# mLSTM cell and exact-GELU feed-forward on one core: y of two batches in chunks three to six turned by VectorE and a way through DRAM, and the down stage's steps in a new order

## The chip, the cores and the metric

The kernel runs on one core of a Trainium2 chip. The core has TensorE (matrix products, PE in the profile), VectorE (DVE), ScalarE (ACT), GpSimd (POOL) and SyncE (SP), whose queue issues nearly all DMAs of this kernel. Each engine works through its own instructions in program order; they wait for one another by semaphores. The metric is the device time of one execution in microseconds, as the median of several runs. A share of the executions is recorded by the hardware profiler, and times of single instructions come from one such execution.

## The reference

An mLSTM cell runs over 768 steps for 4 batches of 8 heads of 40, and its output, 3072 rows of 320, goes through a feed-forward block with an exact GELU.

```python
for t in range(S):
    m_new = np.maximum(f_gate[:, :, t] + m, i_gate[:, :, t])
    f_stab = np.exp(f_gate[:, :, t] + m - m_new)
    i_stab = np.exp(i_gate[:, :, t] - m_new)
    C = f_stab * C + i_stab * einsum(v_t, k_t)
    n = f_stab * n + i_stab * k_t
    denom = np.maximum(np.abs(n . q_t), 1.0)
    y[:, :, t] = sigmoid(o_gate[:, :, t]) * (C q_t) / denom
...
h = x @ w_in                                   # x: (3072, 320), w_in: (320, 2048)
g = 0.5 * h * (1.0 + erf(h * inv_sqrt2))
return g @ w_out                               # w_out: (2048, 320)
```

All data are float32.

## The kernel before

The 768 steps are cut into six chunks of 128, and in each chunk the recurrence is computed in parallel form: scores of queries and keys, weighted by exponentials of the gates, times the values, plus what the state of the chunk before contributes. A chunk of all four batches is 512 tokens, which then go through the feed-forward block together. The product with `w_in` (the *up* stage) takes each float32 operand in parts: `x_hi`, `x_lo` and `x_all` (L499 to L516 make them) against `w_in_hi`, `w_in_lo` and their sum `w_mid`. The product with `w_out` (the *down* stage) is done with seven half-size products instead of eight, each for two tiles of tokens: 14 steps F of eight matrix products (L877).

The program is played from lists of words. After each up stage of chunk c, `DOWN` is played: the 14 steps F of chunk c, with all steps of the cell of chunk c + 1 spread between them. This happens four times, for the cells of chunks three to six (c = 2 to 5 in the code). The cell of chunk two is played within `FRONT`, and after the last up stage there are 14 F alone. The word order is the order of the instructions on every engine's queue. The letters, with the two pairs of batches u = 0, 1 and the two halves j = 0, 1 of a chunk:

- M u: GpSimd masks the loaded gate rows (L530). W b: ScalarE takes their exponentials (L540).
- K b, Q b: VectorE turns keys and queries of batch b by 32x32 blocks (L552); Q also has GpSimd weigh the values (L434). K and Q of batches 0 and 1 are played inside the up stage.
- L 3: GpSimd clears two regions of the old `g` (L149) and SP loads keys and queries of batch 3 there (L159, eight DMAs). j: eight such loads for the next chunk.
- S u: TensorE makes the scores (L588), VectorE multiplies them by the weights (L591).
- r u,j: TensorE reads the state (L602), VectorE multiplies by the decay (L615).
- C u: TensorE makes the state's update (L637). a u,j: GpSimd decays the state (L623). b u,j: VectorE adds the update (L645).
- V u: TensorE multiplies weights and values (L655), into the PSUM banks that C used (tag "a"); VectorE adds the state's part (L666); SP loads the next gate rows (L175), keys and values (L133).
- G b: ScalarE makes the output gate (L417, L419). Y b (`finish`): GpSimd and VectorE gate and normalise y (L475 to L482). For one batch at a time, VectorE then copies the last 64 columns twice into `y_rest` (L488).
- X b (`turn_y`): TensorE turns y in three transposes into the PSUM tile `px` (L499), ScalarE writes `x_hi` (L509), SP loads the next output gates (L138, two DMAs).
- R b (`split_x`): VectorE makes `x_lo` and `x_all` from `px` and `x_hi` (L515, L516).
- N: VectorE's late sums for the down products (L907); F11 to F14 need them. After F's, ScalarE copies (L894, L900) or VectorE adds (L890) the results, and SP sends them out (L862).

The up stage that follows needs `x_hi` of all four batches at once, then `x_lo`, then `x_all`.

Of the kernel before, what the change touches and what calls it, by code (L numbers as in the profile page):

```python
# [9 lines left out]
F32 = mybir.dt.float32  # L10
F32R = mybir.dt.float32r
BF16 = mybir.dt.bfloat16
U32 = mybir.dt.uint32
AF = mybir.ActivationFunctionType
OP = mybir.AluOpType

P = 128

I23 = 2.0 ** 23
PART = 1.0 - 2.0 ** -13  # L20
# [5 lines left out]


FRONT = """w0 L0 t0 w1 L1 O0 O1 P0 k2 E s0 w3 I4 t2 P1 g1 v0 L3 e2 t1 O3 g0 K N D O2 s1 w2 t3 y0 s2 c1 L5 M0 g3 K g2 v1 y1 P2 J Q s3 c0 L4 W0 v2 c3 x0 y2 j1,0 j1,1 x1 P3 O4 J c2 v3 K y3 O5 x2 W1 J A P7 q d P8 P9 x3 a0,0 K J K j0,1 K u0 J G0 j0,0 U J u1 C0 b0,0 O7 r0,0 a0,1 b0,1 H K S0 r0,1 K J K u3 J K L6 J A A J K K J e3 K J K J J K K J K J L7 z J a1,0 A U K J K J K J K j2,0 z K j2,1 O6 J U U h J h p K j3,1 J K J K j3,0 J F F M1 V0 u2 K J W3 h z z h Y0 W2 z z S1 r1,0 C1 z F z F Z G1 b1,0 F F F X0 a1,1 b1,1 G2 Y1 F r1,1 n z V1 F F X1 G3 Y2 R0 R1 Y3 F F X2 R2 F X3 e4 e5 e6 Z F R3"""
DOWN = """F M0 W0 W1 F G2 S0 G1 L3 r0,0 a0,0 C0 K2 M1 b0,0 F W2 F F a0,1 b0,1 K3 r0,1 G0 V0 W3 F Q2 F a1,0 Y0 Y1 Q3 F S1 r1,0 C1 b1,0 X0 F X1 a1,1 R0 b1,1 N j F r1,1 V1 G3 Y2 Y3 R1 F F X2 F X3 R2 F R3"""


@with_exitstack
def kernel(
# [16 lines left out]
    nc = tc.nc  # L50

    B, H, S, D = q.shape
    L = P
# [5 lines left out]
    DM = H * D  # L59
    DFF = moe_w_in.shape[1]  # L60
    NF = DFF // P
    TG = B * L
    R = P // 2
    NX = 2
    NLD = 4
# [10 lines left out]
    raw = ctx.enter_context(tc.tile_pool(name="raw", bufs=2))  # L76
    two = ctx.enter_context(tc.tile_pool(name="two", bufs=2))
    dram = ctx.enter_context(tc.tile_pool(name="dram", bufs=1, space=bass.MemoryType.DRAM))
# [23 lines left out]
    odd_far = blocks[:, H * XB:]  # L102
# [9 lines left out]
    ob = [const.tile([P, DM], F32, name=f"ob{n}") for n in range(NLD)]  # L112
# [3 lines left out]
    f_sb = gates.tile([BH, NCH, L], F32, name="f_sb")  # L116
    i_sb = gates.tile([BH, NCH, L], F32, name="i_sb")
    M_d = dram.tile([NCH - 1, 2, BH, R], F32, name="M_d")

    def out_of(n):  # L120
        return ob[n % NLD].rearrange("p (h d) -> p h d", d=D)

    halves = (slice(0, R), slice(R, P))
    quarters = tuple(slice(R // 2 * n, R // 2 * (n + 1)) for n in range(4))

    def load(n, first=0, end=4):

        if n >= NCH * B:
            return
        c, b = divmod(n, B)  # L130
        for src, dst in ((q, qb), (k, kb), (v, vb), (o_gate, None))[first:end]:
            if dst or c < 1:
                nc.sync.dma_start(out=dst[turn_of(n)][:, :, 0:D] if dst else out_of(n), in_=src[b, :, c * L:(c + 1) * L, :].rearrange("h p d -> p h d"))  # L133
                continue
            u, j = divmod(b, 2)
            t = c * L + R * j
            for i in range(2):
                nc.sync.dma_start(out=out_of(n)[halves[i]], in_=src[2 * u + i, :, t:t + R, :].rearrange("h p d -> p h d"))  # L138
# [24 lines left out]
    def turn_of(n):  # L163

        return n % NLD if n < 2 * B else (n - 2 * B) % NQ
# [214 lines left out]
    def unread(bank):  # L380
        for _ in range(idle[0]):
            nc.tensor.matmul(bank, ident, ident, start=True, stop=True, skip_group_check=True)
        idle[0] = 0
# [4 lines left out]
    class FirstCell:  # L388


        def __init__(self, c):
            self.c = c

            self.engine = nc.gpsimd
            self.finished, self.turned = [], []
            self.qT, self.kT, self.vw, self.far, self.hs, self.px = {}, {}, {}, {}, {}, {}
# [74 lines left out]
        def finish(self, b):  # L471
            n, hs = self.c * B + b, self.hs.pop(b)
            y = out_of(n)
            if self.c > 0:
                nc.gpsimd.tensor_tensor(out=y, in0=hs[:, :, 0:D], in1=y, op=OP.mult)  # L475
            else:
                nc.vector.scalar_tensor_tensor(out=y, in0=y, scalar=1.0, in1=hs[:, :, 0:D], op0=OP.add, op1=OP.mult)
            den = two.tile([P, H], F32, name="den", tag="den", bufs=1)
            nc.vector.tensor_scalar(out=den, in0=hs[:, :, D], scalar1=-1.0, scalar2=None, op0=OP.mult)
            nc.vector.scalar_tensor_tensor(out=den, in0=hs[:, :, D], scalar=1.0, in1=den, op0=OP.max, op1=OP.max)  # L480
            nc.vector.reciprocal(out=den, in_=den)
            nc.vector.scalar_tensor_tensor(out=y, in0=y, scalar=0.5 if self.c < 1 else 1.0, in1=den.unsqueeze(2).to_broadcast([P, H, D]), op0=OP.mult, op1=OP.mult)  # L482
            self.finished.append(b)
            if len(self.finished) == len(self.turned) + 1:
                self.twice(b)
# [3 lines left out]

        def turn_y(self, b):  # L490
            n, t = self.c * B + b, slice(b * L, (b + 1) * L)
            if self.c > 0:
                px = ps_tr.tile([P, NX + 1, L], F32, name="px", tag="tr")
            else:
                px = ps_mm.tile([P, NX + 1, L], F32, name="px", tag="b")
            unread(px[:, 0, :])
            for k in range(NX + 1):
                y = ob[n % NLD][:, k * P:(k + 1) * P] if k < NX else y_rest.rearrange("p two r -> p (two r)")
                nc.tensor.transpose(px[:, k, :], y, ident)  # L499
            self.turned.append(b)  # L500
            if len(self.finished) > len(self.turned):
                self.twice(b + 1)
            if self.c == 0:
                nc.scalar.copy(out=first_x[:, :, t], in_=px)
                return
            self.px[b] = px
            if "x" not in parts:
                parts["x"] = raw.tile([P, NX + 1, TG], F32R, name="x_hi", tag="x", bufs=1)
            nc.scalar.activation(out=parts["x"][:, :, t], in_=px, func=AF.Copy, scale=PART)  # L509
            load(n + NLD, 3, 4)  # L510

        def split_x(self, b):
            px, t = self.px.pop(b), slice(b * L, (b + 1) * L)
            hi = parts["x"][:, :, t]
            nc.vector.scalar_tensor_tensor(out=parts["x_lo"][:, :, t], in0=px, scalar=-1.0 / BASE, in1=hi, op0=OP.mult, op1=OP.add)  # L515
            nc.vector.tensor_tensor(out=parts["x_all"][:, :, t], in0=px, in1=hi, op=OP.subtract)  # L516

# [160 lines left out]
    w_sums, parts, fars, w_hi, w_lo, w_mid = [], {}, [], [], [], {}  # L678
# [261 lines left out]
    def in_turn(steps):  # L940
        todo = list(steps)
        return lambda: todo.pop(0)() if todo else None

    def first_steps(letters):
        cell = FirstCell(0)
        return dict(zip(letters, (cell.weights, cell.gate, cell.turn, cell.scores, cell.carry, cell.values, cell.finish, cell.turn_y)))

    def cell_steps(c, letters, before):
        cell = Cell(c)
        cell.before = before  # L950
        return dict(zip(letters, (cell.mask, cell.weights, cell.gate, cell.scores, cell.update, cell.values,
                                  cell.finish, cell.turn_y, cell.split_x, cell.read, cell.decayed, cell.grown, cell.load_last,
                                  cell.turn_k, cell.turn_q, cell.load_next, cell.first_turn, cell.weigh_values)))

    first_g = Hidden()
    first_products, first_late = down_steps(0, first_g)
    n_pieces = range(len(pieces))
    last_of = lambda c0, c1: by_sub(gg)[:, c0:c1, :, R - 1:R].rearrange("p c j l -> p (c j) l")
    dec_of = lambda c0, c1: dec[:, 2 * (c0 - 1):min(2 * (c1 - 1), 2 * (NCH - 1) - 1)]
    steps = first_steps("wgtscvyx") | cell_steps(1, "MWGSCVYXRrab---pju", first_g)  # L960
    steps |= dict(P=fetch, L=lambda n: load(n, 0, 2), O=lambda n: load(n, 2, 4), e=load_M, E=second_gates,
                  N=later_gates, I=keep_clock, k=warm, D=lambda: gates_turned((ew[:, 0:2], ewT[:, 0:2])),
                  Q=lambda: (gates_turned((ew[:, 2:], ewT[:, 2:])), decays_turned(2, NCH)),
                  d=lambda: (decays_turned(1, 2), decays_last(last_of(1, 2), dec_of(1, 2))),
                  q=lambda: decays_last(last_of(2, NCH)[:, 0:-1], dec_of(2, NCH)),
                  A=in_turn(first_up_steps(0)), U=in_turn(first_up_steps(1)), F=in_turn(first_products), n=first_late,
                  h=in_turn(lambda k=k: hidden_sums(first_g, 2 * k, 2 * k + 2) for k in range(HF // 2)),
                  z=in_turn(lambda w=w: weight_sum(*w) for w in sums),
# [3 lines left out]
    for c in range(1, NCH):  # L972
        g, steps = Hidden(), {}
        if c + 1 < NCH:
            steps = cell_steps(c + 1, "MWGSCVYXRrabLKQj", g)
        up(g, [lambda b=b: (steps["K"](b), steps["Q"](b)) for b in range(2)] if steps else [])
        products, late = down_steps(c, g)
        steps |= dict(F=in_turn(products), N=late)
        play("F " * 14 if c + 1 == NCH else DOWN, steps)

# [29 lines left out]
```

## Time and profile before

| | us |
|---|---|
| runs | 454.77, 455.12, 455.23: median 455.12 |
| the profiled execution, its own time | 453.08 |
| its span, first to last instruction | 451.1 |
| TensorE busy in the span | 444.3 |
| VectorE busy | 301.8 |
| ScalarE busy | 188.7 |
| GpSimd busy | 76.7 |
| all transposes of y by TensorE (72, L499) | 9.6 + 6.6 |
| a down stage, start of its first F to start of the next up stage | 40.0 |

The span is what the profiler records between the first and the last instruction; the execution's time has about 2 us around it. A row of a timeline gives start, duration, engine, line, operation, the tile written and the tiles read, and how many instructions were merged into it. In a row of windows, each engine's busy time is followed by its number of instructions, then come TensorE's granted clock (1.00 is full), the share of the DMA engines that was busy and GB/s. A row of DMA issues gives the number of DMAs, the size of each and the median time in us from issue to landing. TensorE's matrix products overlap and their ends are modelled, so its work is best measured from start to start.

### The profile page before, as it was taken

How to read it: one execution, taken by the hardware profiler on the slowest of the kernel's cores; microseconds unless marked ns; L12 is line 12 of the kernel's file. 1: busy time of each engine (PE TensorE's matmuls, PEld its weight loads, DVE VectorE, ACT ScalarE, POOL GpSimd, SP SyncE). 2: the span in 40 equal slices, each digit the busy share in tenths (PEclk: the TensorE clock that was granted, in tenths of full speed). 3: DMA queues.
4: the chain of work that ended last, by engine and by line, in shares of the span. 5: the costliest groups of instructions: out<-in, count | busy, mean ns of one | idle time of the engine just before them, and what ended most of it. 6: DMA issues, size and time to landing. Idle time of an engine off the chain costs nothing.

```text
span 451.1 us, 12699 instructions
## 1 busy us (share of the span) xinstructions
PE 444.3 (98%) x5256; PEld 394.8 (88%) x5256; DVE 301.8 (67%) x596; ACT 188.7 (42%) x476; POOL 76.7 (17%) x118
## 2 busy tenths in 40 slices
PE   8999999999999999999999999999999999999996
PEld 4897888999878999878999878999877999877996
DVE  4995779897967789645779635779544779532331
ACT  5989597813246811135901134901133911232100
POOL 2222120012200522200522300522200421000000
PEclk9999999999999999999999999999999999999999
DMA  9999999422822257512256522256522300200002
GB/s 157 211 199 229 275 265 227 75 45 57 192 47 55 52 120 150 122 42 51 55 113 148 122 53 51 55 108 118 111 52 51 69 16 3 60 0 1 0 1 58
DMA packets 112808, 43.04 MB, mean 95 GB/s; under 512 B 87600, under 2 KB 107056, under 8 KB 112752
## 3 DMA queue, kind: packets, MB, share of 16 engines
q1 hardware_dynamic: 112432, 41.92, 41.7%
q8 instruction: 41, 0.67, 0.6%
q10 hardware_dynamic: 320, 0.33, 0.2%
q14 instruction: 15, 0.12, 0.1%
HBM read 38.21 MB, written 4.01 MB: 94 GB/s over the span
## 4 chain that ended last, share of the span: by engine, by line
PE 98%; DMA 1%; ACT 0%; DVE 0%; issue 0%; SPq 0%; DVEq 0%; ACTq 0%
PE po L877 41%; PE pu L814 25%; PE pu L825 7%; PE pu L759 6%; PE ps L588 2%; PE pf L602 2%; PE ph L655 2%; PE px L499 2%; PE pu L765 2%; PE pc L637 2%; PE ps L445 1%; PE ph L469 1%; PE pt L570 1%; PE pt L427 1%; DMA i_sb<-in_i_gate_dram 1%; PE pm L409 1%
## 5 line engine op out<-in xcount | busy, mean ns | idle before, releaser
L877 PE MATMUL po<-w_out,g 128*128 128x160 f32 x768 | 111.0, 301 | 0.0
L877 PEld LDWEIGHTS po<-w_out,g 128*128 128x128 f32 x768 | 105.3, 190 | 2.3 <-ACT g L829 1.8
L829 ACT ACTIVATE g<-pu 128x512 f32<-128x512 f32 x80 | 40.9, 617 | 109.3 <-PE pu L825 109.2
L877 PE MATMUL po<-w_sums,sums 128*128 128x160 f32 x384 | 54.6, 300 | 0.0
L877 PEld LDWEIGHTS po<-w_sums,sums 128*128 128x128 f32 x384 | 52.7, 190 | 0.2
L509 ACT ACTIVATE x_hi<-px 128x384 fp32r<-128x384 f32 x20 | 9.8, 492 | 89.0 <-PE px L499 82.4
L814 PE MATMUL pu<-x_hi,w_in_hi 128*128 128x512 f32 x160 | 41.3, 400 | 0.0
L814 PE MATMUL pu<-x_lo,w_in_lo 128*128 128x512 f32 x160 | 40.6, 395 | 0.0
L540 ACT ACTIVATE W<-W,aT 128x64 f32<-128x64 f32 x160 | 40.0, 336 | 0.1
L890 DVE TENSOR_TENSOR o_sb<-po,o_sb 128x320 f32<-128x320 f32 (+1 forms) x32 | 15.0, 469 | 34.6 <-PE po L877 29.7
L746 DVE TENSOR_TENSOR sums<-g 128x512 f32<-128x512 f32 x24 | 16.5, 688 | 31.2 <-ACT g L829 31.2
L814 PEld LDWEIGHTS pu<-x_hi,w_in_hi 128*128 128x128 f32 x160 | 29.4, 188 | 8.0 <-ACT g L829 1.8
L814 PEld LDWEIGHTS pu<-x_lo,w_in_lo 128*128 128x128 f32 x160 | 30.1, 188 | 7.2
L814 PE MATMUL pu<-x_all,w_mid 128*128 128x512 f32 x80 | 31.6, 395 | 0.0
L814 PE MATMUL pu<-x_all,w_in_mid 128*128 128x512 f32 x80 | 31.6, 395 | 0.0
L711 DVE TENSOR_TENSOR w_in_mid<-w_in_hi,w_in_lo 128x512 fp32r<-128x512 f32 x20 | 14.7, 735 | 24.2 <-PE pu L814 24.2
L759 PE MATMUL pu<-first_x,w_in 128*128 128x256 f32 x128 | 28.7, 381 | 0.0
L877 PE MATMUL po<-t,g 128*128 128x160 f32 x192 | 27.9, 299 | 0.0
L530 POOL TENSOR_SCALAR_AFFINE_SELECT W<-W 64x1024 f32<-64x1024 f32 x20 | 24.5, 1227 | 18.9 <-DMA W<-M_d 18.3
L434 POOL TENSOR_TENSOR vw<-vb,ewT 128x328 f32<-128x328 f32 x22 | 16.9, 772 | 59.5 <-DMA vb<-in_v_dram 31.5
L759 PEld LDWEIGHTS pu<-first_x,w_in 128*128 128x128 f32 x128 | 23.9, 190 | 3.4 <-ACT g L769 0.3
L877 PEld LDWEIGHTS po<-t,g 128*128 128x128 f32 x192 | 26.4, 190 | 0.0
(181 smaller groups left out, 722.2 us busy)
## 6 DMA issues: line engine op xcount, KB each, us to landing
W<-M_d SPq DMA_DIRECT2D x20, 256.0 KB, 4.9
bits<-in_moe_w_in_dram SPq DMA_DIRECT2D x14, 256.0 KB, 4.5
kb<-in_k_dram SPq DMA_DIRECT2D x22, 160.0 KB, 4.1
vb<-in_v_dram SPq DMA_DIRECT2D x22, 160.0 KB, 4.1
ob<-in_o_gate_dram SPq DMA_DIRECT2D x40, 80.0 KB, 2.9
bits<-in_moe_w_out_dram SPq DMA_DIRECT2D x10, 320.0 KB, 5.9
out_dram<-o_sb SPq DMA_DIRECT2D x36, 80.0 KB, 2.1
bits_hi<-in_moe_w_out_dram SPq DMA_DIRECT2D x6, 320.0 KB, 5.4
```

What stands on the lines that cost most here:

```text
L434: self.engine.tensor_tensor(out=vw, in0=vb[turn_of(self.c * B + b)], in1=per_head(ewT, self.c, b).to_broadcast([P, H, D1]), op=OP.mult)
L509: nc.scalar.activation(out=parts["x"][:, :, t], in_=px, func=AF.Copy, scale=PART)
L530: nc.gpsimd.affine_select(out=Mb[2 * self.c + u][r], in_=Mb[2 * self.c + u][r], compare_op=OP.is_ge, fill=1.0e30, base=0, pattern=[[0, 2], ...
L540: nc.scalar.activation(out=W[n][:, i, h, :], in_=W[n][:, i, h, :], func=AF.Exp, scale=-1.0, bias=aT[:, self.c, r:r + 1])
L711: nc.vector.tensor_tensor(out=w_mid[i], in0=w_hi[i], in1=w_lo[i], op=OP.add)
L746: nc.vector.tensor_tensor(out=s1, in0=a21, in1=a22, op=OP.add)
L759: nc.tensor.matmul(banks[-1][e][:, i - i0, :], in_tile(i, x)[:, e, i % 2 * P:(i % 2 + 1) * P], first_x[:, x, t0:t1], start=(x == 0 and i = ...
L814: nc.tensor.matmul(pus[i][e], w[k][:, e, i * P:(i + 1) * P], x[:, k, :], start=(n == 0 and k == 0), stop=False, skip_group_check=True)
L825: nc.tensor.matmul(pu[e], w[r, i // 2, i % 2 * P:(i % 2 + 1) * P], x[r, NX, :], start=False, stop=(n == 2), skip_group_check=True)
L829: nc.scalar.activation(out=g.t[:, HF * e + i, :], in_=pu[e], func=AF.Gelu, scale=4097.0)
L877: nc.tensor.matmul(bank[at][:, i, :], lhs(j, t), rhs(j), start=(first and i == 0 and j == 0), stop=(i == n - 1 and j == HF - 1), skip_grou ...
L890: nc.vector.tensor_tensor(out=to, in0=pb, in1=x, op=OP.add)
```

## The change

In the cells of chunks three to six, y of batches 0 and 1 is no longer turned by TensorE. VectorE turns it by 32x32 blocks into a tile that is free by then, four DMAs of SP per batch write it to DRAM such that rows become columns, and a new step B reads both batches back into `x_all`, in three DMAs. `split_x` then has ScalarE make `x_hi` from there, where for the other two batches `turn_y` makes it from `px`; batches 0 and 1 need no `y_rest`. The list `DOWN` is put into a new order, with B 0 in it; `FRONT` stays as it is.

```diff
--- before.py
+++ after.py
@@ -26,7 +26,7 @@
 
 
...
-DOWN = """F M0 W0 W1 F G2 S0 G1 L3 r0,0 a0,0 C0 K2 M1 b0,0 F W2 F F a0,1 b0,1 K3 r0,1 G0 V0 W3 F Q2 F a1,0 Y0 Y1 Q3 F S1 r1,0 C1 b1,0 X0 F X1 a1,1 R0 b1,1 N j F r1,1 V1 G3 Y2 Y3 R1 F F X2 F X3 R2 F R3"""
+DOWN = """M1 M0 a1,0 W0 a0,0 W1 F S0 r0,0 C0 F L3 b0,0 a0,1 F W2 b0,1 F G0 K2 r0,1 W3 V0 K3 G1 Y0 F F F Q2 Q3 X0 S1 Y1 r1,0 X1 C1 b1,0 a1,1 F b1,1 B0 F N F G3 j r1,1 V1 G2 Y2 Y3 F R0 F X2 R1 F X3 R2 R3 F"""
 
 
 @with_exitstack
@@ -116,6 +116,7 @@
     f_sb = gates.tile([BH, NCH, L], F32, name="f_sb")
     i_sb = gates.tile([BH, NCH, L], F32, name="i_sb")
     M_d = dram.tile([NCH - 1, 2, BH, R], F32, name="M_d")
+    y_d = [dram.tile([DM, B, L], F32, name=f"M_dy{n}") for n in range(2)]
 
     def out_of(n):
         return ob[n % NLD].rearrange("p (h d) -> p h d", d=D)
@@ -390,6 +391,7 @@
 
         def __init__(self, c):
             self.c = c
+            self.turns = {}
 
             self.engine = nc.gpsimd
             self.finished, self.turned = [], []
@@ -480,6 +482,9 @@
             nc.vector.scalar_tensor_tensor(out=den, in0=hs[:, :, D], scalar=1.0, in1=den, op0=OP.max, op1=OP.max)
             nc.vector.reciprocal(out=den, in_=den)
             nc.vector.scalar_tensor_tensor(out=y, in0=y, scalar=0.5 if self.c < 1 else 1.0, in1=den.unsqueeze(2).to_broadcast([P, H, D]), op0=OP.mult, op1=OP.mult)
+            if self.c > 0 and b < (0 if self.c < 2 else 2):
+                self.turns[b] = (hs.rearrange("p h d -> p (h d)") if b else odd_far)[:, 0:DM].rearrange("p (f t) -> p f t", t=32)
+                return
             self.finished.append(b)
             if len(self.finished) == len(self.turned) + 1:
                 self.twice(b)
@@ -489,6 +494,15 @@
 
         def turn_y(self, b):
             n, t = self.c * B + b, slice(b * L, (b + 1) * L)
+            if "x" not in parts and self.c > 0:
+                parts["x"] = raw.tile([P, NX + 1, TG], F32R, name="x_hi", tag="x", bufs=1)
+            if b in self.turns:
+                z = self.turns[b]
+                nc.vector.transpose(out=z, in_=ob[n % NLD].rearrange("p (f t) -> p f t", t=32))
+                for r in range(0, P, 32):
+                    nc.sync.dma_start(out=y_d[self.c % 2][:, b, r:r + 32].rearrange("(f i) t -> i f t", i=32), in_=z[r:r + 32])
+                load(n + NLD, 3, 4)
+                return
             if self.c > 0:
                 px = ps_tr.tile([P, NX + 1, L], F32, name="px", tag="tr")
             else:
@@ -504,14 +518,24 @@
                 nc.scalar.copy(out=first_x[:, :, t], in_=px)
                 return
             self.px[b] = px
-            if "x" not in parts:
-                parts["x"] = raw.tile([P, NX + 1, TG], F32R, name="x_hi", tag="x", bufs=1)
             nc.scalar.activation(out=parts["x"][:, :, t], in_=px, func=AF.Copy, scale=PART)
             load(n + NLD, 3, 4)
 
+        def fetch_x(self, u):
+            to = parts["x_all"][:, :, 2 * L * u:2 * L * (u + 1)].bitcast(F32)
+            src = y_d[self.c % 2][:, 2 * u:2 * u + 2].rearrange("d n t -> d (n t)")
+            nc.sync.dma_start(out=to[:, 0:NX, :], in_=src[0:NX * P].rearrange("(k p) t -> p k t", p=P))
+            for r in halves:
+                nc.sync.dma_start(out=to[r, NX, :], in_=src[NX * P:DM])
+
         def split_x(self, b):
-            px, t = self.px.pop(b), slice(b * L, (b + 1) * L)
+            t = slice(b * L, (b + 1) * L)
             hi = parts["x"][:, :, t]
+            if b in self.turns:
+                px = parts["x_all"][:, :, t].bitcast(F32)
+                nc.scalar.activation(out=hi, in_=px, func=AF.Copy, scale=PART)
+            else:
+                px = self.px.pop(b)
             nc.vector.scalar_tensor_tensor(out=parts["x_lo"][:, :, t], in0=px, scalar=-1.0 / BASE, in1=hi, op0=OP.mult, op1=OP.add)
             nc.vector.tensor_tensor(out=parts["x_all"][:, :, t], in0=px, in1=hi, op=OP.subtract)
 
@@ -950,14 +974,14 @@
         cell.before = before
         return dict(zip(letters, (cell.mask, cell.weights, cell.gate, cell.scores, cell.update, cell.values,
                                   cell.finish, cell.turn_y, cell.split_x, cell.read, cell.decayed, cell.grown, cell.load_last,
-                                  cell.turn_k, cell.turn_q, cell.load_next, cell.first_turn, cell.weigh_values)))
+                                  cell.turn_k, cell.turn_q, cell.load_next, cell.fetch_x, cell.first_turn, cell.weigh_values)))
 
     first_g = Hidden()
     first_products, first_late = down_steps(0, first_g)
     n_pieces = range(len(pieces))
     last_of = lambda c0, c1: by_sub(gg)[:, c0:c1, :, R - 1:R].rearrange("p c j l -> p (c j) l")
     dec_of = lambda c0, c1: dec[:, 2 * (c0 - 1):min(2 * (c1 - 1), 2 * (NCH - 1) - 1)]
-    steps = first_steps("wgtscvyx") | cell_steps(1, "MWGSCVYXRrab---pju", first_g)
+    steps = first_steps("wgtscvyx") | cell_steps(1, "MWGSCVYXRrab---pBju", first_g)
     steps |= dict(P=fetch, L=lambda n: load(n, 0, 2), O=lambda n: load(n, 2, 4), e=load_M, E=second_gates,
                   N=later_gates, I=keep_clock, k=warm, D=lambda: gates_turned((ew[:, 0:2], ewT[:, 0:2])),
                   Q=lambda: (gates_turned((ew[:, 2:], ewT[:, 2:])), decays_turned(2, NCH)),
@@ -972,7 +996,7 @@
     for c in range(1, NCH):
         g, steps = Hidden(), {}
         if c + 1 < NCH:
-            steps = cell_steps(c + 1, "MWGSCVYXRrabLKQj", g)
+            steps = cell_steps(c + 1, "MWGSCVYXRrabLKQjB", g)
         up(g, [lambda b=b: (steps["K"](b), steps["Q"](b)) for b in range(2)] if steps else [])
         products, late = down_steps(c, g)
         steps |= dict(F=in_turn(products), N=late)
```

## The prediction

> **What bounds the kernel.** I read the page's busy line and chain of waits first, then the busy times by window of the four down stages that the change touches, then one of these stages instruction by instruction.
>
> ```profile
> PE 444.3 (98%) x5256; PEld 394.8 (88%) x5256; DVE 301.8 (67%) x596; ACT 188.7 (42%) x476; POOL 76.7 (17%) x118
> PE 98%; DMA 1%; ACT 0%; DVE 0%; issue 0%; SPq 0%; DVEq 0%; ACTq 0%
> ```
>
> TensorE is the bound: the chain that ended last runs on it for 98% of the span. The windows show it in the stages themselves:
>
> ```profile
> core 0: us, PE busy (x) PEld busy (x) DVE busy (x) ACT busy (x) POOL busy (x), PEclk, DMA share, GB/s
> 210.51:250.52 40.01, 40.01 (x750) 39.13 (x749) 30.93 (x66) 18.56 (x53) 11.31 (x18) 1.00 0.46 97
> 141.78:181.80 40.02, 40.02 (x751) 39.14 (x749) 30.92 (x66) 18.56 (x53) 11.75 (x18) 1.00 0.50 106
> 279.23:319.24 40.01, 40.01 (x749) 39.07 (x748) 30.92 (x66) 18.53 (x53) 13.70 (x20) 1.00 0.45 94
> 348.03:387.80 39.77, 39.77 (x685) 38.89 (x684) 29.21 (x62) 18.56 (x53) 8.98 (x14) 1.00 0.16 35
> ```
>
> Each stage is 40.0 us long and TensorE is never idle in it, at full clock. So only two things can move the time: TensorE work that goes, and TensorE waits that come. VectorE has 9 us to spare in each stage. The timeline of one stage gives the slots:
>
> ```profile
> 210.51 4.61 PE L877 MATMUL po<-w_out,g 128*128 128x160 f32 x32
> 215.05 1.16 PE L588 MATMUL ps<-qT,kT 40*64 40x64 f32 x64
> 221.73 2.34 PE L877 MATMUL po<-w_out,g 128*128 128x160 f32 x16
> 224.00 0.68 PE L602 MATMUL pf<-state,qT 40*64 40x41 f32 x32
> 224.48 1.12 PE L655 MATMUL ph<-vb,W 64*64 64x41 f32 x64
> 234.48 0.44 PE L499 MATMUL px<-ident,ob 128*128 128x128 f32 x2
> 234.75 0.27 PE L499 MATMUL px<-ident,y_rest 128*128 128x128 f32 x1
> 234.86 2.34 PE L877 MATMUL po<-w_out,g 128*128 128x160 f32 x16
> 237.04 0.38 PE L499 MATMUL px<-ident,ob 128*128 128x128 f32 x2
> 237.26 0.27 PE L499 MATMUL px<-ident,y_rest 128*128 128x128 f32 x1
> 237.37 2.34 PE L877 MATMUL po<-w_out,g 128*128 128x160 f32 x16
> ```
>
> Slots are read from start to start, since ends are modelled: one product step (F) is 221.73 to 224.00 = 2.27 us.
>
> **Removed.** The transposes of two batches (X0, X1): 234.48 to 234.86 = 0.38 and 237.04 to 237.37 = 0.33, so 0.71 us a stage, 4 x 0.71 = **2.84 us**. That is the ceiling of the gain. Two y_rest copies of VectorE (0.23 each) go as well. TensorE's other steps are the same 14 F, S, r, C, V in as many runs (F F | S r C | F F F becomes F | S r C | F F F, and the F that is saved follows the second C in place of the transposes), so the boundaries between shapes cost the same.
>
> **The first half in the new order.** S0 comes after one F, so S0, r0,0, C0, r0,1 and V0 each run 2.27 us earlier. V0 (values, L655) then stands at 224.48 - 2.27 = 222.21. Its two PSUM banks are those that C0 filled, and they come free when the state additions b0,0 and b0,1 (L645) have read them. What these wait for:
>
> ```profile
> 219.47 1.11 DVE L552 STREAM_TRANSPOSE kT<-blocks 128x512 f32<-128x512 f32 x1
> 220.43 1.00 DVE L645 TENSOR_TENSOR state<-state,pc 40x328 f32<-40x328 f32 x2
> 221.61 0.73 POOL L623 TENSOR_TENSOR state<-state,dec 128x328 f32<-128x328 f32 x1 [2.27 <-DVE state L645]
> ```
>
> The chain begins at the score products of VectorE at 217.80, which wait for ScalarE's last exponentials (217.96), and these for the gelus of the up stage: none of it moves. The key transpose K2 does move, behind b0,1, so b0,0 starts at 219.47 and ends at 220.47. GpSimd's decay a0,1 follows 0.18 later (as 221.43 to 221.61 now) and takes 0.73: 221.38. In an earlier stage VectorE went on 0.07 after that decay (153.61 to 153.68), so b0,1 runs 221.45 to 222.45, and V0's second bank is free near 222.5: **a new wait of 0.3 us**. In the last of the four stages the second state is not wanted, there is no b0,1, and the wait is missing: 3 x 0.3 = **0.9 us**. Bounds: 0, if the decay is hidden as now; 0.6, if the 0.18 is paid at every hand-over.
>
> **Queues passed.** Both masks and two decays now head GpSimd's queue (M1, M0, a1,0, a0,0: 4.7 + 1.5 us); they run during the up stage, after the value weighing that waits for its load (250.32 now). There they slow VectorE: one w_mid sum took 1.63 instead of 0.69 beside a mask (252.77). The two urgent sums will be over by then (R3 is played before the last F, which frees VectorE 0.9 us earlier), and the next has 3 us to spare: nothing. L3 (four memsets on GpSimd, eight loads on SP) waits for the second F, to about 217.3 instead of 215; its keys and queries land by 223 and K3, Q3 read them at 225 and 228.4: hidden. SP is free from 220 until V0's loads (M, k, v), which go out 2 us earlier with V0; v of batch 3 lands at 230.8 (232.64 now), its weighing ends at 231.55, and C1's second half wants it at 232.1: hidden by 0.5. Q3's transpose ends near 229.4 and S1 starts at 232.25 - 2.27 + 0.3 = 230.3: hidden by 0.9.
>
> **Added.** Per batch: one 32x32 block transpose of 128x320 (the trace has 128x512 at 1.10, so 0.69; bounds 0.49, a 128x320 addition, and 1.10), four DMAs of 320 pieces of 128 B; then per stage three loads (B0) and two scalings on ScalarE from SBUF instead of PSUM (0.49). Two transposes less two copies add 0.9 us to VectorE's 30.9. SP's issues cost 0.43 to 0.63 (o-gate loads 0.63), so X0 takes SP from 230.2 to 233.8 with the o-gate load behind it. X1's transpose follows S1's products, Y1 and r1,0 and ends at 235.1: its four DMAs issue until 237.2. How long the way through DRAM takes, no row shows. The nearest:
>
> ```profile
> W<-M_d SPq DMA_DIRECT2D x20, 256.0 KB, 4.9
> out_dram<-o_sb SPq DMA_DIRECT2D x36, 80.0 KB, 2.1
> M_d<-M SPq DMA_DIRECT2D x5, 16.0 KB, 2.4
> ```
>
> Writes: 2.0 (the fastest M_d) to 4.1 (the slowest of the k and q block loads); I take 2.2, as the pieces of M_d are nearly as small. Read back: 256 KB from DRAM, 3.4 to 6.6, median 4.9, which I take. The last write issues at 236.7 and lands at 238.9, the fetch goes out behind the o-gate load at 239 and lands at **243.9** (bounds 242.4 and 247.4). SP stands still for at most 2 us before B0; behind it wait j (eight block loads, wanted at 257) and V1's loads (wanted in the next stage): hidden.
>
> **Who waits for the fetch.** ScalarE's scaling in R0, then R0 on VectorE, then behind R0 the p3 addition and the y_rest copy that X3 needs. By the rows VectorE is busy without a break from S1's products (231.6) through b1,1, the late sums (2.35), Y2 and Y3 up to 245.7; R0 (0.93) ends at 246.6, the addition and the copy at 247.2. X3's slot is 248.13 - 0.71 + 0.3 = 247.7. So the fetch may land as late as 245.5, and VectorE has 0.5 us in hand: nothing is lost. R3 ends near 250.2; the up stage starts at 250.1 and wants x_lo 2 us later, x_all 3.9 later.
>
> **Sum.** -2.84 + 0.9 = -1.9 us. The profiled execution took 453.08 (span 451.1, 2.0 around it), so it would take 451.2; it lies 2.0 under the median of the runs, 455.12, which becomes **453.2**. About 0.2% (0.9 us) is what a measurement here can tell from no change.
>
> **Rivals.** (1) V0 does not wait: the full 2.84, 452.3. For it, the decay's hand-over takes only 0.07 once; against it, the chain has no slack left in its own rows. (2) VectorE becomes the bound of the second half: it has 0.5 us in hand before X3. If the block transpose costs 1.10 (+0.4), and the two additions from SBUF are slowed beside GpSimd as the first den row of Y2 is (0.60 instead of 0.17), 0.4 to 0.7 is lost in each of four stages, 1.6 to 2.8: 454.8 to 456.0, no change. Against it: the rows, each taken at what it costs in this very stage. The Trainium skill (VectorE: DVE Perf Modes, Rules for kernel authors) gives 128x128 transposes to TensorE where PSUM will do as destination; by that rule this case is the one to expect, but the windows show TensorE full and VectorE not. (3) **Slower: the way through DRAM is late.** It decides from a landing at 245.5. At the upper bounds the writes land at 240.8 and the fetch at 247.4, with R0's scaling and sums pushing y_rest and X3 by 1.9 us in each stage: +7.6 - 1.9, 460.8; half of that delay gives 457. For it: 2,560 pieces of 128 B in a stage, against pieces of 160 B and more in all of the rows, and SP issuing almost without a break from 230 to 241. Against it: 1,024 pieces of 160 B land in 4.1 us here, and the DMA share of the stage is only 0.46. The Trainium skill (DMA: Bandwidth & Descriptors, Specifications) says that pieces under 512 B are written by read-modify-write; no row here shows 128 B written, and the 256 B pieces of M_d landed in 2.0 to 2.4 us without a sign of it. (4) The change does its work, but something that I don't see, SP's or ScalarE's queue, holds a step: slower by a little.
>
> **How the numbers follow.** Forecast 0.45 (own range 452.6 to 454.1), rival 1 0.13, rival 2 0.17, rival 3 0.22, rival 4 0.03. Faster 0.45 + 0.13 = 0.58; same 0.17; slower 0.25. The range goes from the ceiling's 452.3 less the runs' spread of 0.3, to 457.5, over half of rival 3; about 0.12 lies above it.
>
> **What would show it.** Right: 24 px transposes fewer; down stages near 39.6 us (39.1 the last); V0 waiting about 0.3 us on L645 in three of them; no TensorE wait at S1, C1, X2, X3. Wrong: a wait before X3 or at the start of the up stage that ends on ScalarE's scaling or on the fetch (rival 3), or on VectorE's y_rest copy with the fetch long landed (rival 2); or TensorE's idle time in these stages over 0.7 us each.

## The result, and the profile after

The changed kernel takes 451.82 us in the median of 9 runs (451.16 to 452.81), the kernel before 454.77 us in the 9 runs beside them (452.93 to 458.76): a ratio of 0.9935, with a 95% interval of 0.9907 to 0.9964. The direction is the one forecast, but 451.82 lies just under the range (452.0 to 457.5). A repetition, told below, gave 0.9960 (0.9945 to 0.9975), that is 1.8 us less (1.1 to 2.5), where 1.9 was forecast. So the size of the change was right within what the runs can tell, and the level that it was taken from was not. Two executions are in none of the ratios of this document, since they were far slower than the others of their kernel: one of the kernel before at 1143.76 us and one of the experiment late_fetch at 466.52 us.

The page's busy line and its chain of waits say what they said before: TensorE is the bound (95% of the chain that ended last, 98% before), with 24 instructions less.

```profile
PE 443.1 (98%) x5232; PEld 392.4 (87%) x5232; DVE 308.9 (68%) x596; ACT 187.9 (42%) x476; POOL 81.5 (18%) x118
PE 95%; DMA 1%; ACT 1%; DVE 1%; issue 0%; DVEq 0%; ACTq 0%
```

The windows of the four down stages, from the first F to the up stage, with the columns of the table shown in the prediction:

```profile
211.57:251.30 39.73, 39.73 (x745) 38.84 (x743) 32.05 (x68) 17.16 (x52) 7.42 (x13) 1.00 0.52 107
143.08:182.77 39.69, 39.69 (x744) 38.81 (x743) 32.06 (x68) 17.16 (x52) 7.43 (x13) 1.00 0.57 115
280.08:319.80 39.72, 39.72 (x744) 38.85 (x743) 32.04 (x68) 17.15 (x52) 7.43 (x13) 1.00 0.52 102
348.63:387.91 39.28, 39.28 (x681) 38.40 (x679) 30.51 (x64) 17.16 (x52) 5.51 (x10) 1.00 0.26 53
```

Start to start, the stages took 40.0, 40.0, 40.1 and 39.9 us before, 160.0 in all; now 158.4. VectorE has 1.1 us more to do in each of the first three and 1.3 in the last, GpSimd less, since both masks and two decays now run in the up stage.

TensorE in the second of these stages, from its timeline:

```profile
211.57 2.44 PE L901 MATMUL po<-w_out,g 128*128 128x160 f32 x16
213.94 1.16 PE L612 MATMUL ps<-qT,kT 40*64 40x64 f32 x64
223.37 1.44 PE L679 MATMUL ph<-vb,W 64*64 64x41 f32 x64
224.75 4.61 PE L901 MATMUL po<-w_out,g 128*128 128x160 f32 x32
233.69 2.44 PE L901 MATMUL po<-w_sums,sums 128*128 128x160 f32 x16
235.97 4.51 PE L901 MATMUL po<-w_out,g 128*128 128x160 f32 x32
246.40 0.38 PE L513 MATMUL px<-ident,ob 128*128 128x128 f32 x2
```

The first is the first F (one F is x16, since the profile lists two instructions for each of its eight products), the second S0. Lines of the changed kernel have other numbers than before: L901 is the old L877, L679 the old L655, L513 the old L499. V0 (L679) takes 223.37 to 224.75 = 1.38, where it took 224.48 to 225.53 = 1.05 before: this is the new wait of 0.3. Behind the second C, at 233.69, an F follows at once where X0 stood; its slot is 2.28. X2 starts at 246.40.

The rows of VectorE, GpSimd and ScalarE behind these:

```profile
220.49 1.00 DVE L669 TENSOR_TENSOR state<-state,pc 40x328 f32<-40x328 f32 x2
221.64 0.73 POOL L647 TENSOR_TENSOR state<-state,dec 128x328 f32<-128x328 f32 x1 [2.54 <-DVE state L669]
222.41 1.00 DVE L669 TENSOR_TENSOR state<-state,pc 40x328 f32<-40x328 f32 x2 [0.92 <-POOL state L647]
244.96 0.52 ACT L536 ACTIVATE x_hi<-x_all 128x384 fp32r<-128x384 f32 x1 [13.41 <-DMA x_all<-M_dy]
246.67 0.55 DVE L539 SCALAR_TENSOR_TENSOR x_lo<-x_all,x_hi 128x384 fp32r<-128x384 f32 x1
248.14 0.22 DVE L493 COPY y_rest<-ob 128x128 f32<-128x128 f32 x1
```

b0,0, the decay a0,1 and b0,1 follow one another without a gap of use, and b0,1 ends at 223.41. Of V0's 64 instructions only two start ahead of that or with it (223.37 and 223.43), the next at 223.56. The last DMA of the fetch has landed at 244.86, and ScalarE makes x_hi at 244.96; VectorE gets to R0 only at 246.67, so nobody on the path waits for it. The copy that X3 needs ends at 248.36, X3 reads it at 249.12.

The DMAs of the way through DRAM (number, size of each, median us to landing):

```profile
x_all<-M_dy SPq DMA_DIRECT2D x4, 256.0 KB, 4.2
M_dy<-blocks SPq DMA_DIRECT2D x16, 40.0 KB, 2.1
M_dy<-far SPq DMA_DIRECT2D x16, 40.0 KB, 1.7
x_all<-M_dy SPq DMA_DIRECT2D x8, 64.0 KB, 4.4
```

### The profile page after: what moved, and what is told of

Its sections match the earlier page's. It is cut to its first block, busy times and chain, and to the rows that moved or that the text cites. A ratio compares the mean times of both kernels' runs of the same rounds, so it can differ in the third digit from the quotient of the medians.

```text
span 451.0 us, 12699 instructions
## 1 busy us (share of the span) xinstructions
PE 443.1 (98%) x5232; PEld 392.4 (87%) x5232; DVE 308.9 (68%) x596; ACT 187.9 (42%) x476; POOL 81.5 (18%) x118
## 4 chain that ended last, share of the span: by engine, by line
PE 95%; DMA 1%; ACT 1%; DVE 1%; issue 0%; DVEq 0%; ACTq 0%
PE po L901 42%; PE pu L838 25%; PE pu L849 7%; PE pu L783 6%; PE ps L612 2%; PE ph L679 2%; PE pf L626 2%; PE pu L789 2%; PE pc L661 2%; PE px L513 1%; ACT W L415 1%; DMA kb<-in_k_dram 1%; PE pt L594 1%; PE ps L447 1%; PE ph L471 1%; PE pt L429 1%
## 5 line engine op out<-in xcount | busy, mean ns | idle before, releaser
L901 PE MATMUL po<-w_out,g 128*128 128x160 f32 x768 | 110.8, 302 | 0.0
L901 PEld LDWEIGHTS po<-w_out,g 128*128 128x128 f32 x768 | 105.2, 190 | 2.5 <-ACT g L853 1.8
L853 ACT ACTIVATE g<-pu 128x512 f32<-128x512 f32 x80 | 40.8, 616 | 54.6 <-PE pu L849 54.4
L901 PE MATMUL po<-w_sums,sums 128*128 128x160 f32 x384 | 55.2, 300 | 0.0
L901 PEld LDWEIGHTS po<-w_sums,sums 128*128 128x128 f32 x384 | 52.9, 190 | 0.2
L838 PE MATMUL pu<-x_lo,w_in_lo 128*128 128x512 f32 x160 | 40.7, 396 | 0.0
L735 DVE TENSOR_TENSOR w_in_mid<-w_in_hi,w_in_lo 128x512 fp32r<-128x512 f32 x20 | 16.3, 813 | 21.1 <-PE pu L838 21.1
L554 POOL TENSOR_SCALAR_AFFINE_SELECT W<-W 64x1024 f32<-64x1024 f32 x20 | 26.0, 1299 | 21.9 <-DMA W<-M_d 21.1
L783 PE MATMUL pu<-first_x,w_in 128*128 128x256 f32 x128 | 28.7, 381 | 0.0
L901 PE MATMUL po<-t,g 128*128 128x160 f32 x192 | 27.9, 299 | 0.0
L901 PEld LDWEIGHTS po<-t,g 128*128 128x128 f32 x192 | 26.4, 190 | 0.0
```

Source lines behind the costliest of these rows:

```text
L554: nc.gpsimd.affine_select(out=Mb[2 * self.c + u][r], in_=Mb[2 * self.c + u][r], compare_op=OP.is_ge, fill=1.0e30, base=0, pattern=[[0, 2], ...
L735: nc.vector.tensor_tensor(out=w_mid[i], in0=w_hi[i], in1=w_lo[i], op=OP.add)
L783: nc.tensor.matmul(banks[-1][e][:, i - i0, :], in_tile(i, x)[:, e, i % 2 * P:(i % 2 + 1) * P], first_x[:, x, t0:t1], start=(x == 0 and i = ...
L838: nc.tensor.matmul(pus[i][e], w[k][:, e, i * P:(i + 1) * P], x[:, k, :], start=(n == 0 and k == 0), stop=False, skip_group_check=True)
L853: nc.scalar.activation(out=g.t[:, HF * e + i, :], in_=pu[e], func=AF.Gelu, scale=4097.0)
L901: nc.tensor.matmul(bank[at][:, i, :], lhs(j, t), rhs(j), start=(first and i == 0 and j == 0), stop=(i == n - 1 and j == HF - 1), skip_grou ...
```

## The experiments

The theory after the result (A): the gain is made in the down stages, 1.6 us there; what the first medians show beyond it is scatter ahead of the stages, where FRONT is the same in both kernels. In the profiled executions the first F of the first stage stands at 141.8 us before and at 143.1 after, so the one that was profiled after had lost 1.3 us ahead of the change. The rival (B): the change does something there too. Each kernel is compared with the kernel before, run on the same chip beside it: same_again, turn_only, order_only and b00_first on one chip, the other four on another. The first F is that of the first of the four stages; the stages and up stages are those of one profiled execution each.

| kernel | ratio (95% interval) | first F | four down stages, us | up stages |
|---|---|---|---|---|
| same_again | 1.0000 (0.9990 to 1.0011) | 142.2 | 40.0, 40.0, 40.4, 39.9 | 28.7 |
| after_again | 0.9960 (0.9945 to 0.9975) | 142.3 | 39.7, 39.7, 39.7, 39.3 | 28.8 |
| turn_only | 1.0007 (0.9990 to 1.0024) | 142.0 | 40.4, 40.1, 39.9, 39.2 | 28.7 |
| order_only | 1.0061 (1.0047 to 1.0075) | 142.4 | 40.7, 40.8, 41.1, 40.4 | 28.8 |
| b00_first | 0.9955 (0.9944 to 0.9967) | 142.1 | 39.6, 39.5, 39.6, 39.4 | 28.8 |
| early_table | 0.9947 (0.9931 to 0.9964) | 142.2 | 39.6, 39.5, 39.6, 39.4 | 28.7 |
| late_fetch | 1.0147 (1.0105 to 1.0190) | 141.9 | 42.7, 42.7, 41.0, 39.4 | 28.8 |
| more_vector | 1.0039 (1.0023 to 1.0056) | 143.6 | 40.7, 40.8, 40.8, 39.3 | 28.8 |

**The two kernels again (same_again, after_again).** No edit.

> The kernel before, unchanged. Theory A (the gain is made in the four down stages): the ratio to before is 1.000, its runs spread over some 2 us, and its profiled execution has the four down stages at 40.0, 40.0, 40.0 and 39.8 us, as in the first profile; whatever moves between two executions moves ahead of the first down stage (its first F at 141.8 us in the first profile of before, 143.1 in that of the changed kernel, though the two play the same FRONT). Rival B (part of the gain is made ahead of the first down stage, by something that the change does there): the first F stands at 142.5 or later in most executions of this kernel, and earlier than that in most of the changed one's.

> The changed kernel once more, unchanged. Theory A (the gain is what the four down stages show, 1.6 us, less 0.3 that the up stages lose; the rest of the 2.95 between the first medians is scatter ahead of the stages, where the profiled execution of the changed kernel lost 1.2 us to a wait for a load of keys): ratio 0.996 to 0.998, and in its profile the stages again at 39.7, 39.7, 39.7 and 39.3 us with the first F at about 142. Rival (2.95 is the size of the gain): ratio 0.9935.

The medians of the kernel before were 453.53 (11 runs, the repetition), 453.82 (23 runs, beside it) and 454.25 (13 runs, on the other chip); the changed kernel had 452.02 (7 runs). The first F stands between 141.8 and 143.6 in all ten profiled executions: 141.8 and 142.2 in the two of the kernel before, 143.1 and 142.3 in the two of the changed one. Rival B, which wanted it later before than after, falls as far as two executions of each can show. The first ratio, 0.9935, held an excess that did not come back; the two intervals overlap from 0.9945 to 0.9964. One part of theory A did not hold: the third stage of same_again has 40.4 instead of 40.1, for a break of 0.26 in its products at 289.08 that waits for nothing the profile shows. So one stage of one execution can be off by 0.3 by itself.

**The turn without the new order (turn_only).** The old list, with only the steps that the way through DRAM needs elsewhere:

```diff
-... Q3 F S1 r1,0 C1 b1,0 X0 F X1 a1,1 R0 b1,1 N j F r1,1 V1 G3 Y2 Y3 R1 F F X2 F X3 R2 F R3
+... Q3 F X0 S1 r1,0 X1 C1 b1,0 F a1,1 b1,1 B0 N j F r1,1 V1 G3 Y2 Y3 F R0 F X2 R1 F X3 R2 R3 F
```

> The turn by VectorE and DRAM with the steps of before in their old order; X0, X1, R0, R1 and B0 alone are put where their data allow it. Theory A: V0 has no new wait, the 24 transposes are gone (0.71 us a stage), but VectorE has one product step less between S1 and X2, so that the y_rest copies are late for X2 and X3 by some 0.6 us in all: stages of about 39.9, so 0.4 us (0.1%) faster than before as a whole. If the turn alone makes the gain, and the order nothing: stages of 39.3, 2.8 us (0.6%) faster. If the way through DRAM needs the new order: slower than before.

The stages came out at 39.9 in the mean, as expected: 159.6 in all, 0.4 less than before, which runs spread from 452.1 to 456.1 cannot show; their ratio is that of no change. Rows of ScalarE, VectorE and TensorE in the first stage, and of VectorE and TensorE in the second, say why:

```profile
177.88 0.52 ACT L536 ACTIVATE x_hi<-x_all 128x384 fp32r<-128x384 f32 x1 [17.06 <-DMA x_all<-M_dy]
178.43 0.56 DVE L539 SCALAR_TENSOR_TENSOR x_lo<-x_all,x_hi 128x384 fp32r<-128x384 f32 x1 [0.52 <-ACT x_hi L536]
180.17 0.33 PE L513 MATMUL px<-ident,y_rest 128*128 128x128 f32 x1 [0.60 <-DVE y_rest L493]
247.26 0.56 DVE L539 SCALAR_TENSOR_TENSOR x_lo<-x_all,x_hi 128x384 fp32r<-128x384 f32 x1 [0.24 <-ACT x_hi L536]
249.00 0.33 PE L513 MATMUL px<-ident,y_rest 128*128 128x128 f32 x1 [0.32 <-DVE y_rest L493]
```

X3 waits for VectorE's copy, and VectorE has two reasons to be late with it. One is the fetch: VectorE stands idle at R0 for x_hi, which waits for the fetch, 0.52 us in the first stage and 0.24 in the second. X3's last transpose comes 0.75 and 0.48 late there, counted from 0.22 behind the start of its first two. What is left, 0.23 and 0.24, is VectorE's own, and in the third stage, where it does not wait for x_hi, X3 is late by 0.26 as well. So the turn alone frees TensorE and then makes it wait, partly for the way through DRAM (rival 3 of the prediction), partly for VectorE (rival 2). The new order mends both: it gives VectorE one product step more between S1 and X2, and the fetch goes out 27.9 us behind the stage's first F instead of 32.1 (239.44 and 243.23 in the second stage).

**The order without the turn (order_only).** DOWN in the new order, all four batches turned by TensorE, no B0:

```diff
-            if self.c > 0 and b < (0 if self.c < 2 else 2):
+            if self.c > 0 and b < 0:
...
-... Q2 Q3 X0 S1 Y1 r1,0 X1 C1 b1,0 a1,1 F b1,1 B0 F N F G3 j r1,1 V1 G2 Y2 Y3 F R0 F X2 R1 F X3 R2 R3 F
+... Q2 Q3 S1 Y1 r1,0 C1 b1,0 a1,1 X0 F X1 b1,1 R0 F N F G3 j r1,1 V1 G2 Y2 Y3 R1 F F X2 F X3 R2 R3 F
```

> The new order with TensorE's transposes for all four batches, X0 and X1 behind C1 and R0, R1 behind them, no way through DRAM. Theory A: the order alone only costs, namely the wait at V0 (0.3 us in three stages) and the product run split after its first F (0.1 in each): stages of 40.4, 1.3 us (0.3%) slower than before. If the order makes part of the gain: at or under before's 40.0.

```profile
223.72 1.46 PE L679 MATMUL ph<-vb,W 64*64 64x41 f32 x64
237.20 0.33 PE L513 MATMUL px<-ident,y_rest 128*128 128x128 f32 x1 [0.21 <-DVE y_rest L493]
```

The order alone costs, and more than expected: 3.0 us over the four stages instead of 1.3. V0's wait is there (1.46). The rest is a second wait of 0.4, at X1, whose slot is 236.61 to 237.37 instead of 0.33: there y_rest comes behind VectorE's other work. That one is owed to where X0 and X1 stand in this kernel, so the order's own price is not measured cleanly; that it is no gain by itself, with X0 and X1 where they stand here, is.

**V0's wait (b00_first).** The changed kernel with one step moved:

```diff
-... F S0 r0,0 C0 F L3 b0,0 a0,1 F ...
+... F S0 C0 b0,0 r0,0 F L3 a0,1 F ...
```

> The changed kernel with the state addition b0,0 played ahead of r0,0 (C0 b0,0 r0,0 in place of r0,0 C0 ... b0,0), so that GpSimd's decay a0,1 and b0,1 come 0.47 us earlier. Theory A: V0's wait of 0.3 us goes in three stages: stages of 39.45, 0.9 us (0.2%) faster than the changed kernel. Rival (V0 is long for another reason, the exponentials or the score products): V0's rows stay at 1.4 us, no gain.

```profile
153.88 1.27 PE L679 MATMUL ph<-vb,W 64*64 64x41 f32 x64
222.23 1.16 PE L679 MATMUL ph<-vb,W 64*64 64x41 f32 x64
```

V0's rows went from 1.41 and 1.44 to 1.27 and 1.16, and the first three stages to 39.6, 39.5, 39.6: 0.5 us less in all, not 0.9. So b0,1 is what V0 waited for, for the most part; a remainder of 0.1 to 0.2 in the first and third stages has another cause that stays open (in the first, b0,1 had ended 0.4 us ahead of V0, at 152.44 + 1.00). In the last stage, which has no b0,1, the move costs 0.15. The gain of 0.4 that is left is read from the traces; the runs' intervals for this kernel and the changed one overlap.

**The gelu table (early_table).** ScalarE's rows at the first gelus behind the second stage, in the kernel before (the first two), in the changed kernel (the next two) and in the kernel below (the last two):

```profile
249.16 1.28 ACT L829 ACT_TABLE_LOAD   x1
262.89 4.03 ACT L829 ACTIVATE g<-pu 128x512 f32<-128x512 f32 x8 [12.44 <-PE pu L825]
263.69 1.28 ACT L853 ACT_TABLE_LOAD   x1 [13.77 <-PE pu L849]
264.98 4.03 ACT L853 ACTIVATE g<-pu 128x512 f32<-128x512 f32 x8
248.56 1.28 ACT L855 ACT_TABLE_LOAD   x1
262.33 4.03 ACT L853 ACTIVATE g<-pu 128x512 f32<-128x512 f32 x8 [12.27 <-issue]
```

In the changed kernel the load of the gelu table waits with the first gelu for TensorE, 13.8 us, and the gelus start 13.7 us behind the start of the up stage (251.30). In the kernel before, the load ran at 249.16, right behind the last x_hi, and the gelus started 12.4 us behind the start of the up stage (250.52), when their products were ready. One line on top of b00_first, ahead of the up stage's work (the last line shown is the old one behind it). Its only new work is a gelu of 128x1 into a copy that is not needed any more:

```diff
+        nc.scalar.activation(out=y_rest[:, 0, 0:1], in_=ident[:, 0:1], func=AF.Gelu)
         b0 = pair(0, lambda: split_to(4))
```

> The changed kernel with b0,0 ahead of r0,0 as before, and besides one gelu of a single column at the start of each up stage (its result is thrown away), so that ScalarE loads the gelu table there and not when the first products are ready. Theory A: the first eight gelus come 1.3 us earlier and the up stages are back at 28.7 us, so 0.2 to 0.3 us faster than b00_first: ratio to before 0.995. Rival (the table load is hidden anyway): no difference to b00_first, up stages of 28.78 as there.

The gelus start 12.4 us behind the start of the up stage again (249.92), and the up stages are back at 28.70 to 28.72 us (28.77 to 28.82 without it), 0.3 us over the four. The median is 451.35 beside 452.02 for the changed kernel on the same chip. Against b00_first, which had 451.37 on the other chip, the gain of 0.3 shows in the traces alone.

**The fetch's room (late_fetch).** B0 behind j:

```diff
-... b1,1 B0 F N F G3 j r1,1 ...
+... b1,1 F N F G3 j B0 r1,1 ...
```

> The changed kernel with B0 played behind j, so that the fetch goes out behind the eight block loads of the next chunk, 4.9 us later. Theory A (the fetch has little room: it lands at 244.9 in the second stage, and R0 takes it up at 246.7): ScalarE's x_hi of batch 0 at 249.8 instead of 245, the y_rest copy for X3 some 3.5 us late, each stage 3.5 us longer, 14 us (3%) slower than the changed kernel. Rival (the fetch has room to spare): no difference.

ScalarE and TensorE in its second stage:

```profile
251.55 0.52 ACT L536 ACTIVATE x_hi<-x_all 128x384 fp32r<-128x384 f32 x1 [18.16 <-DMA x_all<-M_dy]
253.84 0.33 PE L513 MATMUL px<-ident,y_rest 128*128 128x128 f32 x1 [2.73 <-DVE y_rest L493]
```

The stage is 3.0 us longer, and the chain is the one expected: fetch, x_hi, R0, the y_rest copy, X3. In all it is 7.4 us in the stages (two of the three runs had 458.9 us, the third 463.6), half of what was expected, because the last stage plays no j (there is no next chunk), so nothing is moved there, and in the third the wait is 1.3.

**VectorE's room (more_vector).** One block transpose played four times:

```diff
-                nc.vector.transpose(out=z, in_=...)
+                for _ in range(4 if b else 1):
+                    nc.vector.transpose(out=z, in_=...)
```

> The changed kernel with the block transpose of batch 1 made four times over, 1.26 us more for VectorE in the stretch from S1 to X3. Theory A (VectorE has some 0.6 us in hand there): X3, and perhaps X2, wait for y_rest, each stage 0.6 to 0.7 us longer, 2.6 us (0.6%) slower than the changed kernel. Rival (VectorE is far from the bound): no difference; rival (VectorE is the bound there already): 1.26 us in each stage, 5.0 us slower.

```profile
237.04 2.14 DVE L502 STREAM_TRANSPOSE far<-ob 128x320 f32<-128x320 f32 x4
248.59 0.44 PE L514 MATMUL px<-ident,ob 128*128 128x128 f32 x2 [0.53 <-DVE ob L484]
```

The four transposes into one tile take 239.11 - 237.04 = 2.07 where one takes 0.42, so 1.65 us were added, not 1.26. The first three stages grew by 1.0: about 0.65 of the 1.65 was taken up. VectorE has that much in hand, and it is X2 that waits first, for Y2's result. The last stage, without b1,1, took up all of it.

## Why the prediction was right or wrong

**The level, wrong.** The step that failed is the one behind the sum: the profiled execution "lies 2.0 under the median of the runs, 455.12, which becomes 453.2", and the low end that was built on it, "the ceiling's 452.3 less the runs' spread of 0.3". Three runs within 0.5 us of each other were taken for the level of the kernel and for its spread. Nine runs beside the changed kernel, those three among them, still gave 454.77; the later sets of runs gave 453.53, 453.82 and 454.25, so the level was 0.9 to 1.6 us too high, and single runs went from 452.5 to 458.8. From 453.5 to 454.3, the forecast of 1.9 less is 451.6 to 452.4; the changed kernel had 451.8 and 452.0. Why the kernel before was slower in its first set of runs stays open. And the distance of a profiled execution from the median does not carry over: it was 2.0 below before, and 1.0 above after (452.81 against 451.82), where 1.3 us had been lost ahead of the first F.

**The size, right, with some luck.** Against the first profile of the kernel before, the repetition of the changed kernel gained 1.55 us in the four down stages, 0.35 less than forecast, and lost 0.3 in the up stages. It gained 0.4 where nothing had been forecast: 0.2 at the very end, behind VectorE's last addition, which ends 31.06 us behind the start of the last 14 F in both, and 0.2 outside the span (452.02 - 450.2 = 1.8, where the kernel before has 2.0). turn_only has the gain at the end and order_only the one outside the span; what makes them is open. That adds up to 1.6 or 1.7, within the 1.1 to 2.5 of the runs.

**Removed, 2.84: too much by 0.4.** The transposes are gone, but the F behind C1 now takes 2.28 where it took 2.18 behind the transposes (234.86 to 237.04). So 0.1 of their slot stays, as the price of the change of shapes after C1: the F behind V0 took 2.28 as well (225.53 to 227.81 in the kernel before); "the boundaries between shapes cost the same" held for the number of runs only.

**V0's wait, 0.3 in three stages: right**, in size and place, and for the most part in cause. The chain b0,0, a0,1, b0,1 took about the times forecast (start to start 1.15 and 0.77, forecast 1.18 and 0.80), and moving it made V0 shorter.

**Down stages: right within 0.2.** 39.6 and 39.1 were forecast, 39.7 and 39.3 measured. -2.84 + 0.4 + 0.9 = -1.5, and the stages show -1.6.

**Queues passed: right in the stages, one miss beside them.** L3, V0's loads, j and the masks hid as forecast. Not foreseen: the gelu table's load, 0.1 us in each up stage, 0.3 to 0.4 in all. It is found with the new order (order_only has it, turn_only does not); what in the order makes it wait, the runs do not tell apart.

**Rival 1** (no wait at V0) falls by V0's rows. **Rival 2** (VectorE becomes the bound) falls, though it was near: VectorE's room of 0.5 us was measured as 0.65, and the turn in the old order shows what happens without it: some 0.25 us of delay at X3 in three stages. The block transpose costs 0.49 (0.42 start to start), the lower bound, not the 0.69 taken; the sums from SBUF cost 0.14 more for each batch than from PSUM (246.67 to 247.74, against 0.93). The Trainium skill (VectorE: DVE Perf Modes, Rules for kernel authors) sends 128x128 transposes to TensorE when PSUM will do; here the measurement says otherwise: the time is 0.4% less with two of four batches turned by VectorE, where TensorE is the engine without room, though only in an order that leaves VectorE room.

**Rival 3** (the way through DRAM is late) was rightly described and did not come. In the second stage the fetch landed at 244.9, 33.3 us behind the stage's first F, where 33.4 was forecast (243.9, with the first F at 210.51), and VectorE took it up at 246.7. The experiment with the late fetch shows that its chain is real, at up to 3.0 us a stage, and turn_only shows a mild form of it. One of its readings was too good: the five M_d writes of 16 KB landed in 2.0 to 3.8 us, with 2.4 as their median, not in 2.0 to 2.4. The Trainium skill (DMA: Bandwidth & Descriptors, Specifications) has pieces under 512 B written by read-modify-write; the 40 KB writes in pieces of 128 B landed in 1.7 to 2.1 us (medians), beside 2.1 for 80 KB of output in rows of 1280 B. No run here has the same bytes in longer pieces, so a price of it is neither shown nor ruled out; it cost the kernel nothing, since nobody waited for the fetch.

## What to carry to other kernels

When one engine has no gap at all, work off that engine is worth its slots, less what the neighbours then pay at their own borders; before it is moved, write out the queue of the engine that takes it, since here the same move gave next to nothing until the steps around it were put in an order that leaves that engine 0.6 us of room and sends the data out 4 us earlier. A trip through DRAM of four writes of 40 KB and some 190 KB back for each batch was free where its data landed 1.7 us ahead of their use, and a later start of the fetch cost up to 3 us a stage. The median of one set of runs is not a level, of three runs or of nine: take several sets, or forecast the difference and compare on one chip.

## What the runs showed of the hardware

- ScalarE loads a function table in 1.28 us, and where the load stands behind the wait of the function's first use, it is paid after the wait: 13.8 us of idle time ahead of it did not hide it. A gelu of one column played earlier took the load with it.
- A block transpose of 128x320 float32 on VectorE takes 0.49 us, as an addition of that size does; repeated into the same tile, each took 0.52 from start to start.
- x_lo and x_all from SBUF operands took 1.07 us together, from PSUM 0.93.
- The same fetch of 256 KB landed in 2.7 to 5.3 us, the fastest in the last stage, where the DMA share is 0.26 instead of 0.52 to 0.57. That the share makes the difference is not shown: in turn_only, where it goes out some 4 us later in the stage, it landed in 2.7 to 3.0 us in all four, at shares of 0.44 to 0.46 and 0.26.
